# Laying the weights' word operations one a step in a fused attention, gate and mixing kernel

## Chip, cores and metric

The kernel runs on one core of a Trainium2 chip. The metric is the device time of one execution in microseconds, as the median of several runs. One profiled execution stands beside them, and every row below is from it.

## What is computed

Three blocks, one behind the other, on a batch of 2 with 768 positions. The change lies in the first, whose work includes preparing weights for the second.

```python
# attention, 8 heads of 64: rows see only keys of their own hash bucket
mask = q_bucket[:, :, :, None] == k_bucket[:, :, None, :]
scores = np.where(mask, scale * q @ k.T, -1e9)
attn = softmax(scores) @ v
# gate: 5 taps along the sequence, conv_w of 5 x 512; w_val, w_out 512 x 512
gate = sigmoid(sum(conv_w[k] * xp[:, k:k + S, :] for k in range(5)))
x = gate * (x @ w_val) @ w_out
# mixing: the real part of a 2-D DFT, a layer norm, an MLP of 512 x 2048 x 512
u = x + real(fft(fft(x, axis=1), axis=2))
out = u + relu(norm(u) @ w_ch1) @ w_ch2
```

The weights arrive as 64-bit floats. The kernel makes of each a high part of fewer bits and a low part, both 32-bit, with integer operations on the two 32-bit words of each number; these are called word operations here.

## The kernel before, in words

**Pairs and steps.** The attention walks over 8 pairs (batch, two heads). A pair has 12 steps, one for each tile of 128 query rows of its two heads, so the loop at L811 has `NT` = 96 steps `n` and two more, with `p, i = divmod(n, 12)`. A step issues, in this order: six transposes of the softmax tile `n` (`p_transpose`, L593), on some steps with two q/k transposes of a later pair beside them (`beside`, L701); the four matmuls of the scores of tile `n + 3` (L557); their clamp with the row minimum on VectorE (L568); the tile's high part on ScalarE (L601) and its low part on VectorE (L605), and the q/k low part (L709) if q/k stood beside; the products with the values (`pv`, L616); the exponential of tile `n + 2` on ScalarE (L575); and then small work: bits of the hash buckets in steps 4 and 5 (L443, L453, L454), copies of outputs on odd steps (L631), values and the convolution on GpSimd.

**What sets the order.** Nothing is rescheduled: each engine takes its instructions in the order in which this loop writes them, so a piece of small work stands where the loop calls it, and everything behind it on its engine waits. The scores have one PSUM tile (`pss`, L310), so the scores of one step can be written only when the clamp of the step before has read them.

**The word operations.** `words_split` (L262) prepares a half of a 128-row chunk of `w_val` (`val_weights`, L785) or of `w_out`'s first chunk (`out_half`, L797), 128 x 256 numbers. It makes five calls, `step0` to `step4`: two operations on VectorE (L271, L272); one (L275); one on ScalarE (L278) and two on VectorE (L279, L280); one on VectorE (L283); one on ScalarE (L286). Their PSUM tile comes from `psm`, which has one buffer and also serves the bits and the conv weights' transpose. The loop (L884 to L890) lays one call a step on steps 6 to 10 of a pair; on steps 7 to 11 in pair 0, and on 0 to 4 in the last. The halves of `w_out` follow in the last pair, steps 5 to 10 (L897 to L908). Each also starts the load of the next `w_val` half (`val_load`).

**The conv weights.** `conv_weights` (L759) converts the 20 x 128 numbers of `conv_w` in the first steps and adds the two parts on VectorE (`whole`, L769); `turn` transposes them on TensorE (L773) and copies them out on VectorE (L774). `CW` (L33) says the step of each of its eight calls.

Of the kernel before, what the change touches and what calls it, by code (L numbers as in the profile page):

```python
# [13 lines left out]
ALU = mybir.AluOpType  # L14
# [15 lines left out]
KSCALE = -0.125  # L30
BIG = 2.0 ** 33

CW = (2, 3, 4, 4, 5, 6, 7, 12)  # L33

WARM = (18, 3, 4)
CLAMP = BIG / 4
# [68 lines left out]
def block_kernel(  # L105
# [4 lines left out]
    nc = tc.nc  # L110
# [65 lines left out]
    def run(steps):  # L176
        for x in steps:
            x()
# [38 lines left out]
    def val_matmul(b, a, c, pv_):  # L217
        xh, xl = xsplit[b, a]
        n = 0
        for w, x in ((wvh, xh), (wvl, xh), (wvh, xl)):  # L220
            for ic in range(NC):
                nc.tensor.matmul(  # L222
                    pv_, w[:, ic, c * P : (c + 1) * P], x[:, ic, :],
                    start=n == 0, stop=n == 3 * NC - 1,
                )
                n += 1
# [33 lines left out]
    wo_raw, wo_h, wo_l = {}, [None] * NC, [None] * NC  # L260

    def words_split(raw, dst_h, dst_l, b, a, g):  # L262

        n = raw.shape[1]
        words = raw.bitcast(I32).rearrange("p (n two) -> p n two", two=2)
        lo, hi = words[:, :, 0], words[:, :, 1]
        a, g = a.bitcast(I32), g.bitcast(I32)
        e = ap4.tile([P, DM], I32, tag="cve", name="cv")[:, :n]

        def step0():  # L270
            nc.vector.tensor_scalar(a, hi, 0x7FFFFE00, None, op0=ALU.bitwise_and)  # L271
            nc.vector.tensor_scalar(g, hi, 0x1FF, 15, op0=ALU.bitwise_and, op1=ALU.logical_shift_left)  # L272

        def step1():
            nc.vector.scalar_tensor_tensor(g, lo, 17, g, op0=ALU.logical_shift_right, op1=ALU.bitwise_or)  # L275

        def step2():
            nc.scalar.activation(a, a, AF.Relu, scale=8.0, bias=col[:, b : b + 1])  # L278
            nc.vector.scalar_tensor_tensor(a, hi, -(2 ** 31), a, op0=ALU.bitwise_and, op1=ALU.bitwise_or)  # L279
            nc.vector.tensor_scalar(e, a, -(2 ** 23), None, op0=ALU.bitwise_and)  # L280

        def step3():
            nc.vector.scalar_tensor_tensor(dst_l, g, 2.0 ** -35, e.bitcast(F32), op0=ALU.mult, op1=ALU.mult)  # L283

        def step4():
            nc.scalar.copy(dst_h, a.bitcast(F32))  # L286

        return [step0, step1, step2, step3, step4]

    def half_weights(raw, dst_h, dst_l, b):  # L290
        t = psm.tile([P, DM], F32, tag="m", name="cvp")
        n = DM // 2
        return words_split(raw, dst_h, dst_l, b, t[:, :n], t[:, n:])
# [8 lines left out]
    def attention(es):  # L302
# [10 lines left out]
        NPR = len(pairs)  # L313
# [47 lines left out]
        def qk_tile(i, pl=ap3):  # L361
            return pl.tile([P, 2, S], F32R, tag=f"qk{i}", name="qk")
# [396 lines left out]
        def conv_weights():  # L759
            cwr, cwh, cwl, cw = cws  # L760
            
            def words_of(n, x):
                c0 = (2 + "aeg".index(x)) * P
                return conv_tmp[:, c0 : c0 + n].bitcast(I32)

            steps = from64(words_of, cwr, lambda: (cwh, cwl), parts=20)

            def whole():
                nc.vector.tensor_tensor(cw, cwh, cwl, op=ALU.add)  # L769

            def turn():
                cwp = psm.tile([P, HS], F32, tag="m", name="cwp")
                nc.tensor.transpose(cwp[:, :20], cw, ident[:20, :20])  # L773
                nc.vector.tensor_copy(cwt, cwp[:, :20].rearrange("p (k c) -> p k c", k=5))  # L774

            return steps + [whole, turn]
# [3 lines left out]
        def val_load(i):  # L780
            c, h = divmod(i, 2)
            wv_raw[i] = ap4.tile([P, DM // 2], I64, tag="wvr", name="wvr", bufs=2)
            nc.sync.dma_start(wv_raw[i], w_val[c * P : (c + 1) * P, h * DM // 2 : (h + 1) * DM // 2])

        def val_weights(i):  # L785
            c, h = divmod(i, 2)
            cs = slice(h * DM // 2, (h + 1) * DM // 2)
            return half_weights(wv_raw[i], wvh[:, c, cs], wvl[:, c, cs], 3)

        def out_tile(i):  # L790
            t = qk_tile((0, 2, 1)[i]).rearrange("p a s -> p (a s)")
            for x in range(3):
                c, part = divmod(3 * i + x, 2)
                if c < NC:
                    (wo_h, wo_l)[part][c] = t[:, x * DM : (x + 1) * DM]

        def out_half(i):  # L797
            cs = slice(i * DM // 2, (i + 1) * DM // 2)
            return half_weights(wo_raw[0][:, cs], wo_h[0][:, cs], wo_l[0][:, cs], 4)
# [3 lines left out]
        def val_early(n, early):  # L803
            c = n - NT + 3
            tail.append(early[:, c % 2, :HS])
            val_matmul(0, 0, c, tail[c])

        convs = [(b, c, i) for b, c in pairs[: NPR - 1] for i in range(9)]
        start()
        NT = 12 * NPR  # L810
        for n in range(NT + 2):  # L811
            p, i = divmod(n, 12)
# [32 lines left out]
            if p + 1 < NPR:  # L845
                prep_step(p + 1, i)
            if n == CW[0]:
                conv = conv_weights()
            run(conv.pop(0) for x in CW if x == n)
            if i == 2 and p + 2 < NPR:  # L850
# [4 lines left out]
            last = p == NPR - 1  # L855
# [25 lines left out]
            elif n == NT - 2:  # L881
                norm_spread(p)

            at = 0 if last else 7 if p == 0 else 6  # L884
            if p < NPR and at <= i < at + 5:
                if i == at:
                    wsteps = val_weights(p)
                    if p + 1 < NPR:
                        val_load(p + 1)
                wsteps[i - at]()  # L890
            for _ in range(1 if n >= NT - 16 else 5 * n // 6 - 5 * (n - 1) // 6):
                if convs and n < NT and n >= min(12 * (4 * convs[0][0] + convs[0][1]) + 22, NT - 6):
                    conv_pool(*convs.pop(0), conv_tmp)
            if p == 6 and i in (2, 6):
                out_load(i // 6)

            if last and i == 5:  # L897
                for x in range(2):
                    out_tile(x)
                osteps = out_half(0)  # L900
            elif last and i == 9:
                osteps = out_half(1)
                osteps.pop(0)()
            if last and 5 <= i < 11:
                osteps.pop(0)()
                if i in (8, 10):
                    run(osteps)
                    osteps = []  # L908
            if p == 5 and i == 9:
                again(pool_copy, 0, slice(0, NC))  # L910
            elif last and i == 6:
# [8 lines left out]
            if NT - 3 <= n < NT + 1 and n != NT - 1:  # L920
                val_early(n, early)
# [20 lines left out]
    with ExitStack() as es:  # L942
        ps, late, convs = attention(es)
# [70 lines left out]
    def mixing(es):  # L1014
# [53 lines left out]

        def chunk(c):
            a, g_ = (x.tile([P, DM], F32, tag=y, name="cvp") for x, y in ((psm, "m"), (pso, "o")))  # L1070
            return words_split(wo_raw[c], wo_h[c], wo_l[c], 4, a, g_)

        def gated(c):
            gate(0, 1, c, late[c], stay=True)
# [5 lines left out]
        for c in range(3):  # L1080
            x_low(1, 0, c)
        w = chunk(1)
        w[0]()
        w[1]()
# [19 lines left out]
        for x in convs:  # L1104
            conv_pool(*x, xT[0][:, 3, :S])
        w = chunk(2)
        w[0]()
        w[1]()
# [325 lines left out]
```

## Time and profile before

| what | us |
|---|---|
| median of 3 runs | 617.57 |
| lowest and highest | 617.46, 617.91 |
| the profiled execution | 617.87 |
| its span | 616.1 |
| TensorE busy in the span | 604.9 |
| VectorE busy | 444.3 |
| ScalarE busy | 358.7 |
| GpSimd busy | 264.8 |

The span is the time between the first and the last instruction; what lies around it is 1.8 us here. A busy TensorE is not TensorE at its peak, since matmuls overlap and their ends are modelled: in the rows a group of transposes or scores lasts into the next group, so the spacing of starts is what to read. Idle time of an engine counts only where another waits for it.

### The profile page before, as it was taken

To read this page: it belongs to the slowest core of one execution; us is meant where nothing else is said; L and a number is where in the kernel's file an instruction comes from. 1 tells how busy PE (TensorE), PEld (TensorE's weight loads), DVE (VectorE), ACT (ScalarE), POOL (GpSimd) and SP (SyncE) were. 2 spreads that over 40 slices of the span, in tenths; PEclk is the share of its full clock that TensorE was granted. 3 is DMA by queue.
4 is the path that set the end of the run, shared out by engine and by line. 5 is a ranking of instruction groups with operands and counts; after the bars stand their busy time and mean duration, and the time that the engine had idled before them with its cause. 6 is when DMAs were issued, how large, how long until landed. Compare 5 with 4: busy or idle time off the path is not lost.

```text
span 616.1 us, 10295 instructions
## 1 busy us (share of the span) xinstructions
PE 604.9 (98%) x3711; PEld 538.6 (87%) x3711; DVE 444.3 (72%) x850; ACT 358.7 (58%) x712; POOL 264.8 (43%) x273
## 2 busy tenths in 40 slices
PE   8999999999999999999999999999999999999997
PEld 7889999999999899998899888888888888888885
DVE  4999999999999997998669787888885411111113
ACT  5988899998999887844624355555665111111121
POOL 7241669687888798792350633233321000000000
PEclk9999999999999999999999999999999999999999
DMA  6966676768686720261100244343440200000002
GB/s 133 215 151 155 162 155 163 164 155 184 153 190 167 174 70 19 73 231 69 41 29 2 68 138 132 108 136 118 126 133 1 103 0 1 1 0 1 1 1 103
DMA packets 52557, 62.01 MB, mean 101 GB/s; under 512 B 28704, under 2 KB 39304, under 8 KB 52250
## 3 DMA queue, kind: packets, MB, share of 16 engines
q1 hardware_dynamic: 51770, 57.81, 36.9%
q0 software_dynamic: 432, 3.55, 1.5%
q8 instruction: 29, 0.48, 0.4%
q14 instruction: 22, 0.18, 0.1%
q10 hardware_dynamic: 304, 0.01, 0.0%
HBM read 36.73 MB, written 3.19 MB: 65 GB/s over the span
## 4 chain that ended last, share of the span: by engine, by line
PE 81%; DVE 14%; issue 2%; ACT 2%; DMA 1%; POOL 0%; SPq 0%; DVEq 0%; ACTq 0%; POOLq 0%
PE pf L1341 20%; PE acc L1351 20%; PE sp L557 9%; PE op L616 8%; PE ptp L593 7%; PE ps L1158 4%; DVE ptl L605 3%; DVE sd L568 3%; PE ps L222 3%; PE ps L1222 3%; PE bp L443 1%; PE late L222 1%; PE ptp L701 1%; PE ps L1193 1%; PE early L222 1%
## 5 line engine op out<-in xcount | busy, mean ns | idle before, releaser
L1351 PE MATMUL acc<-w,hid 128*128 128x512 f32 x576 | 137.4, 391 | 0.0
L1351 PEld LDWEIGHTS acc<-w,hid 128*128 128x128 f32 x576 | 105.5, 188 | 20.1
L1344 DVE SCALAR_TENSOR_TENSOR hid<-pf,hid 128x512 fp32r<-128x512 f32 (+1 forms) x62 | 33.4, 556 | 120.6 <-ACT hid L1343 120.6
L1341 PE MATMUL pf<-uth,w 128*128 128x512 f32 (+1 forms) x496 | 97.2, 337 | 0.1
L568 DVE TENSOR_SCALAR_CACHE_REDUCE sd<-sp 128x768 f32<-128x768 f32 x96 | 91.3, 952 | 7.4 <-PE sp L557 6.9
L1343 ACT ACTIVATE hid<-pf 128x512 fp32r<-128x512 f32 (+1 forms) x62 | 28.9, 488 | 115.2 <-PE pf L1341 115.2
L557 PE MATMUL sp<-qk 128*128 128x512 f32 (+1 forms) x384 | 91.4, 360 | 4.5 <-DVE sd L568 3.7
L605 DVE TENSOR_TENSOR ptl<-ptp,pth 128x768 fp32r<-128x768 f32 x96 | 91.5, 953 | 4.2 <-ACT pth L601 3.8
L1341 PEld LDWEIGHTS pf<-uth,w 128*128 128x128 f32 x496 | 78.9, 188 | 15.6 <-DVE hid L1344 1.9
L575 ACT ACTIVATE sd<-sd,nm 128x768 f32<-128x768 f32 x96 | 90.2, 940 | 1.5 <-DVE sd L568 1.5
L601 ACT CAST pth<-ptp 128x768 fp32r<-128x768 f32 x96 | 77.1, 803 | 17.7 <-PE ptp L701 8.7
L593 PE MATMUL ptp<-ident,sd 128*128 128x128 f32 x576 | 78.5, 272 | 0.2 <-ACT sd L575 0.2
L162 POOL TENSOR_TENSOR w<-cv 128x512 fp32r<-128x512 f32 x31 | 40.4, 1302 | 88.7 <-DVE cv L157 74.4
L616 PE MATMUL op<-pth,v 128*128 128x256 f32 x288 | 73.7, 282 | 0.2 <-ACT xc L631 0.2
L616 PE MATMUL op<-ptl,v 128*128 128x256 f32 x288 | 73.7, 286 | 0.0
L557 PEld LDWEIGHTS sp<-qk 128*128 128x128 f32 x384 | 58.2, 189 | 14.2 <-DVE sd L568 7.9
L593 PEld LDWEIGHTS ptp<-ident,sd 128*128 128x128 f32 x576 | 65.8, 140 | 1.1 <-ACT sd L575 0.5
L616 PEld LDWEIGHTS op<-pth,v 128*128 128x128 f32 x288 | 54.2, 188 | 4.5 <-ACT xc L631 0.4
L616 PEld LDWEIGHTS op<-ptl,v 128*128 128x128 f32 x288 | 54.2, 188 | 0.3
L1341 PE MATMUL pf<-utl,w 128*128 128x512 f32 (+1 forms) x248 | 53.1, 335 | 0.0
L241 POOL TENSOR_TENSOR g<-g,conv_tmp 128x768 f32<-128x768 f32 x27 | 46.7, 1728 | 1.6
L149 ACT ACTIVATE cv<-cv,col 128x512 int32<-128x512 int32 x32 | 23.2, 725 | 40.3 <-DVE cv L146 40.3
(214 smaller groups left out, 984.9 us busy)
## 6 DMA issues: line engine op xcount, KB each, us to landing
raw<-in_moe_w_ch_dram SPq DMA_DIRECT2D x32, 512.0 KB
qk<-ht SPq DMA_DIRECT2D x60, 192.0 KB
qk<-lt SPq DMA_DIRECT2D x30, 192.0 KB
rqk<-in_q_dram SPq DMA_DIRECT2D x16, 192.0 KB
rqk<-in_k_dram SPq DMA_DIRECT2D x16, 192.0 KB
rv<-in_v_dram SPq DMA_DIRECT2D x8, 384.0 KB
out_dram<-o SPq DMA_DIRECT2D x12, 256.0 KB
xm<-xc SPq DMA_DIRECT2D x15, 192.0 KB
```

The costliest lines, as they stand in the source:

```text
L162: nc.gpsimd.tensor_tensor(dst()[1], fold(g.bitcast(F32)), fold(e.bitcast(F32)), op=ALU.mult)
L241: nc.gpsimd.tensor_tensor(dst, dst, tmp, op=ALU.add)
L557: nc.tensor.matmul(sp[:, cs], q2[i][:, m, qi * P : (qi + 1) * P], k2[i][:, m, cs], start=m == order[0], stop=m == order[1])
L568: nc.vector.tensor_scalar(sd[n], sp, CLAMP, None, op0=ALU.min, op1=ALU.min, accum_out=st[p]["nm"][:, n % 12 : n % 12 + 1],)
L575: nc.scalar.activation(sd[n], sd[n], AF.Exp, bias=st[p]["nm"][:, i : i + 1], scale=-1.0, accum_out=st[p]["sums"][:, i : i + 1],)
L593: nc.tensor.transpose(tp[:, r // 3, c0 : c0 + P], sd[n][:, r * P : (r + 1) * P], ident)
L601: nc.scalar.copy(p_parts(n)[0], tp)
L605: nc.vector.tensor_tensor(lo, tp, f32(ho), op=ALU.subtract)
L616: nc.tensor.matmul(po[kb], v3[:, r, c0 : c0 + P], pt[kb][x][:, r, :], start=r == 0 and x == 0, stop=r == R - 1 and x == 1,)
L1341: nc.tensor.matmul(pf, w[:, c, :], x[:, c, cs], start=n == 0, stop=n == 3 * NC - 1)
L1344: nc.vector.scalar_tensor_tensor(hl[:, cs], pf, 0.0, f32(hh)[:, cs], op0=ALU.max, op1=ALU.subtract)
L1351: nc.tensor.matmul(acc, x[:, ts_], w, start=f == 0 and n == 0, stop=f == NF - 1 and n == 2)
```

## The change

`words_split` returns its eight operations by name in place of five calls. In the attention they are laid by a table: for each half a list of steps and names. Halves 1 to 5 begin in step 5 of their pair and end in step 13, which is step 1 of the next pair: `magnitude` 5, `rebias` and `rest` 6, `rest_low` 7, `sign` 8, `high` 10, `exponent` 12, `low` 13. Half 0 goes from step 7 to step 14. Halves 6 and 7 and the two of `w_out` follow each other from step 77 to step 94, one operation of VectorE a step, with the last `w_out` half pressed into two steps. `rebias` (ScalarE) now stands ahead of `rest`, and `high` (ScalarE) ahead of `exponent` or `low` where both are in one step. The later chunks of `w_out`, behind the attention, keep the five calls (`in_five`).

The addition of the conv weights moves from VectorE to GpSimd, and their transpose from step 12 to step 15.

```diff
-CW = (2, 3, 4, 4, 5, 6, 7, 12)
+CW = (2, 3, 4, 4, 5, 6, 7, 15)
...
-        def step2():
+        def rebias():
             nc.scalar.activation(a, a, AF.Relu, scale=8.0, bias=col[:, b : b + 1])
+
+        def sign():
             nc.vector.scalar_tensor_tensor(a, hi, -(2 ** 31), a, op0=ALU.bitwise_and, op1=ALU.bitwise_or)
...
+    def in_five(steps):
+        groups = ("magnitude", "rest"), ("rest_low",), ("rebias", "sign", "exponent"), ("low",), ("high",)
+        return [lambda x=x: run(steps[k] for k in x) for x in groups]
...
             def whole():
-                nc.vector.tensor_tensor(cw, cwh, cwl, op=ALU.add)
+                nc.gpsimd.tensor_tensor(cw, cwh, cwl, op=ALU.add)
...
+        words = [
+            [(7, "magnitude"), (8, "rebias rest"), (9, "rest_low"), (11, "sign"), (12, "exponent"), (13, "low"), (14, "high")]
+        ]
+        for p in range(1, NPR - 2):
+            words.append(
+                [(12 * p + i, x) for i, x in (
+                    (5, "magnitude"), (6, "rebias rest"), (7, "rest_low"), (8, "sign"), (10, "high"), (12, "exponent"), (13, "low"),
+                )]
+            )
+        for n in (12 * NPR - 19, 12 * NPR - 13):
+            words.append(
+                [(n + i, x) for i, x in enumerate(
+                    ("magnitude", "rebias rest", "rest_low", "sign", "high exponent", "low")
+                )]
+            )
+        n = 12 * NPR - 7
+        words.append(
+            [(n + i, x) for i, x in enumerate(("magnitude", "rebias rest", "rest_low", "sign", "high exponent low"))]
+        )
+        words.append([(n + 4, "magnitude rest"), (n + 5, "rebias rest_low sign exponent high low")])
...
-            at = 0 if last else 7 if p == 0 else 6
-            if p < NPR and at <= i < at + 5:
-                if i == at:
-                    wsteps = val_weights(p)
-                    if p + 1 < NPR:
-                        val_load(p + 1)
-                wsteps[i - at]()
+            words_step(n)
...
-            if last and i == 5:
-                for x in range(2):
-                    out_tile(x)
-                osteps = out_half(0)
-            elif last and i == 9:
-                osteps = out_half(1)
-                osteps.pop(0)()
-            if last and 5 <= i < 11:
-                osteps.pop(0)()
-                if i in (8, 10):
-                    run(osteps)
-                    osteps = []
```

**VectorE, pair 1, before.** The words start behind step 6's low part (`ptl`) and go to step 9; `sd` is a clamp, `lt` a q/k low part, `cvp`, `cv` and `wvl` are word operations. Names in brackets are what a row waits for.

```order
L271 TENSOR_SCALAR cvp<-wvr 128x256 [waits DVE_49]
L272 TENSOR_SCALAR cvp<-wvr 128x256 [waits DVE_49]
L568 TENSOR_SCALAR sd,nm<-sp 128x768 [waits PE_49]
L605 TENSOR_TENSOR ptl<-ptp,pth 128x6x128 [waits Activation_49]
L275 SCALAR_TENSOR_TENSOR cvp<-wvr,cvp 128x256 [waits DVE_49]
L568 TENSOR_SCALAR sd,nm<-sp 128x768 [waits PE_49]
L605 TENSOR_TENSOR ptl<-ptp,pth 128x6x128 [waits Activation_49]
L279 SCALAR_TENSOR_TENSOR cvp<-wvr,cvp 128x256 [waits Activation_49]
L280 TENSOR_SCALAR cv<-cvp 128x256 [waits DVE_49]
L568 TENSOR_SCALAR sd,nm<-sp 128x768 [waits PE_49]
L605 TENSOR_TENSOR ptl<-ptp,pth 128x6x128 [waits Activation_49]
L709 SCALAR_TENSOR_TENSOR lt<-ptp,col,ht 128x256 [waits DMAHW7_49,DMAHW0_49]
```

The same place of the change, from step 5's comparison of bits (L467) to step 8's `sign` (L283):

```order
L467 TENSOR_TENSOR bits<-bp,bits 64x384 [waits Activation_49]
L271 TENSOR_SCALAR cvp<-wvr 128x256 [waits DVE_49]
L581 TENSOR_SCALAR sd,nm<-sp 128x768 [waits PE_49]
L618 TENSOR_TENSOR ptl<-ptp,pth 128x6x128 [waits Activation_49]
L274 TENSOR_SCALAR cvp<-wvr 128x256 [waits Activation_49]
L581 TENSOR_SCALAR sd,nm<-sp 128x768 [waits PE_49]
L618 TENSOR_TENSOR ptl<-ptp,pth 128x6x128 [waits Activation_49]
L277 SCALAR_TENSOR_TENSOR cvp<-wvr,cvp 128x256 [waits DVE_49]
L581 TENSOR_SCALAR sd,nm<-sp 128x768 [waits PE_49]
L618 TENSOR_TENSOR ptl<-ptp,pth 128x6x128 [waits Activation_49]
L283 SCALAR_TENSOR_TENSOR cvp<-wvr,cvp 128x256 [waits DVE_49]
```

No two word operations stand between two clamps any more; the second, `rest` (L274), waits for ScalarE, where its forerunner L272 waited for VectorE.

**ScalarE, steps 92 to 94, before.** `pth` is a high part of a softmax tile, `sd` an exponential, `xc` an output copy; the two L286 are the high parts of the `w_out` halves.

```order
L601 CAST pth<-ptp 128x6x128 [waits PE_49,Activation_49]
L575 ACTIVATE sd,sums<-sd,nm 128x768 [waits DVE_49]
L286 CAST qk<-cvp 128x256 [waits DMAHW6_49,DMAHW7_49,DMAHW3_49,DVE_49]
L601 CAST pth<-ptp 128x6x128 [waits PE_49]
L575 ACTIVATE sd,sums<-sd,nm 128x768 [waits Activation_49]
L631 COPY xc<-op 128x256 [waits DMAHW5_49,PE_49,Pool_49]
L601 CAST pth<-ptp 128x6x128 [waits PE_49,Activation_49]
```

The same place of the change:

```order
L614 CAST pth<-ptp 128x6x128 [waits PE_49,Activation_49]
L588 ACTIVATE sd,sums<-sd,nm 128x768 [waits DVE_49]
L614 CAST pth<-ptp 128x6x128 [waits PE_49]
L588 ACTIVATE sd,sums<-sd,nm 128x768 [waits DVE_49,Activation_49]
L644 COPY xc<-op 128x256 [waits DMAHW5_49,PE_49,Pool_49]
L292 CAST qk<-cvp 128x256 [waits DMAHW6_49,DMAHW7_49,DMAHW3_49,DVE_49]
L614 CAST pth<-ptp 128x6x128 [waits PE_49,Activation_49]
```

The `w_out` high part (now L292) went behind the next softmax tile, its exponential and the output copy.

## Rows read from the trace of the kernel before

**Rows 1.** Busy us by engine in two stretches; then TensorE's clock, DMA share, GB/s.

```profile
core 0: us, PE busy (x) PEld busy (x) DVE busy (x) ACT busy (x) POOL busy (x), PEclk, DMA share, GB/s
90.00:120.00 30.00, 29.71 (x228) 28.14 (x227) 28.69 (x54) 27.05 (x57) 24.21 (x24) 1.00 0.72 161
...
203.00:238.00 35.00, 34.14 (x253) 31.58 (x252) 33.81 (x66) 29.66 (x59) 31.01 (x28) 1.00 0.41 100
```

**Rows 2.** The chain of waits, one pair: start us, us on the chain, what.

```profile
91.06 0.96 DVE ptl L605
92.02 0.35 DVE cvp L271
...
92.39 0.43 DVE cvp L272
...
93.73 0.97 PE sp L557 x4
...
120.52 0.35 DVE cvp L271
```

**Rows 3.** Timeline of TensorE, transposes of steps: start us, us, engine, line, operation.

```profile
90.57 0.82 PE L593 MATMUL ptp<-ident,sd 128*128 128x128 f32 x6
...
92.63 0.82 PE L593 MATMUL ptp<-ident,sd 128*128 128x128 f32 x6
...
95.30 0.82 PE L593 MATMUL ptp<-ident,sd 128*128 128x128 f32 x6
...
97.58 0.82 PE L593 MATMUL ptp<-ident,sd 128*128 128x128 f32 x6
...
104.51 0.82 PE L593 MATMUL ptp<-ident,sd 128*128 128x128 f32 x6
```

**Rows 4.** Timeline of VectorE in the same pair.

```profile
92.72 0.95 DVE L568 TENSOR_SCALAR_CACHE_REDUCE sd<-sp 128x768 f32<-128x768 f32 x1
...
93.59 0.95 DVE L605 TENSOR_TENSOR ptl<-ptp,pth 128x768 fp32r<-128x768 f32 x1
94.46 0.42 DVE L275 SCALAR_TENSOR_TENSOR cvp<-wvr,cvp 128x256 int32<-128x256 int32 x1
94.79 0.95 DVE L568 TENSOR_SCALAR_CACHE_REDUCE sd<-sp 128x768 f32<-128x768 f32 x1
...
96.54 0.42 DVE L279 SCALAR_TENSOR_TENSOR cvp<-wvr,cvp 128x256 int32<-128x256 int32 x1
96.99 0.42 DVE L280 TENSOR_SCALAR cv<-cvp 128x256 int32<-128x256 int32 x1
...
99.08 0.47 DVE L709 SCALAR_TENSOR_TENSOR lt<-ptp,col,ht 128x256 fp32r<-128x256 f32 x1
99.47 0.41 DVE L283 SCALAR_TENSOR_TENSOR wvl<-cvp,cv 128x256 fp32r<-128x256 int32 x1
```

**Rows 5.** Timelines of TensorE and VectorE in pair 0, steps 8 to 14.

```profile
34.27 0.82 PE L593 MATMUL ptp<-ident,sd 128*128 128x128 f32 x6
...
47.29 0.23 PE L773 MATMUL cwp<-ident,cwr 20*128 20x20 f32 x1
...
49.80 0.82 PE L593 MATMUL ptp<-ident,sd 128*128 128x128 f32 x6
...
35.74 0.71 DVE L769 TENSOR_TENSOR cwr<-cwr 20x128 f32<-20x128 f32 x1
```

**Rows 6.** Timeline of VectorE, first and last of fifteen clamps, steps 78 to 92.

```profile
204.06 0.96 DVE L568 TENSOR_SCALAR_CACHE_REDUCE sd<-sp 128x768 f32<-128x768 f32 x1 [0.22 <-PE sp L557]
...
236.09 0.95 DVE L568 TENSOR_SCALAR_CACHE_REDUCE sd<-sp 128x768 f32<-128x768 f32 x1
```

**Rows 7.** Timelines of ScalarE and TensorE, steps 92 to 94; idle before in brackets.

```profile
238.28 0.37 ACT L286 CAST qk<-cvp 128x256 fp32r<-128x256 f32 x1 [1.63 <-DVE qk L283]
...
240.59 0.38 PE L616 MATMUL op<-pth,v 128*128 128x256 f32 x1 [0.19 <-ACT xc L631]
```

**Rows 8.** Timeline of ScalarE: an exponential in step 6 of a pair, a `rebias`.

```profile
90.11 0.94 ACT L575 ACTIVATE sd<-sd,nm 128x768 f32<-128x768 f32 x1
...
222.66 0.43 ACT L278 ACTIVATE cvp<-cvp,col 128x256 int32<-128x256 int32 x1
```

More of the change, by code (lines that the diff above doesn't have):

```diff
@@ L268, in words_split, with magnitude, rest, rest_low @@
         e = ap4.tile([P, DM], I32, tag="cve", name="cv")[:, :n]
-        def step0():
+        def magnitude():
             nc.vector.tensor_scalar(a, hi, 0x7FFFFE00, None, op0=ALU.bitwise_and)
+        def rest():
             nc.vector.tensor_scalar(g, hi, 0x1FF, 15, op0=ALU.bitwise_and, op1=ALU.logical_shift_left)
-        def step1():
+        def rest_low():
             nc.vector.scalar_tensor_tensor(g, lo, 17, g, op0=ALU.logical_shift_right, op1=ALU.bitwise_or)
-        def step2():
+        def rebias():
             nc.scalar.activation(a, a, AF.Relu, scale=8.0, bias=col[:, b : b + 1])
+        def sign():
             nc.vector.scalar_tensor_tensor(a, hi, -(2 ** 31), a, op0=ALU.bitwise_and, op1=ALU.bitwise_or)
+        def exponent():
             nc.vector.tensor_scalar(e, a, -(2 ** 23), None, op0=ALU.bitwise_and)
-        def step3():
+        def low():
             nc.vector.scalar_tensor_tensor(dst_l, g, 2.0 ** -35, e.bitcast(F32), op0=ALU.mult, op1=ALU.mult)
-        def step4():
+        def high():
             nc.scalar.copy(dst_h, a.bitcast(F32))
-        return [step0, step1, step2, step3, step4]
+        return dict(
+            magnitude=magnitude, rest=rest, rest_low=rest_low, rebias=rebias, sign=sign, exponent=exponent,
+            low=low, high=high,
+        )
+    def in_five(steps):
+        groups = ("magnitude", "rest"), ("rest_low",), ("rebias", "sign", "exponent"), ("low",), ("high",)
+        return [lambda x=x: run(steps[k] for k in x) for x in groups]
     def half_weights(raw, dst_h, dst_l, b):
@@ L806, in val_early, with words_step @@
             val_matmul(0, 0, c, tail[c])
+        words = [
[16 more added lines that the diff above has]
+            [(n + i, x) for i, x in enumerate(("magnitude", "rebias rest", "rest_low", "sign", "high exponent low"))]
+        )
+        words.append([(n + 4, "magnitude rest"), (n + 5, "rebias rest_low sign exponent high low")])
+        parts = {}
+        def words_step(n):
+            for i, plan in enumerate(words):
+                for at, names in plan:
+                    if at != n:
+                        continue
+                    if at == plan[0][0]:
+                        if i == NPR:
+                            for x in range(2):
+                                out_tile(x)
+                        parts[i] = val_weights(i) if i < NPR else out_half(i - NPR)
+                        if i + 1 < NPR:
+                            val_load(i + 1)
+                    run(parts[i][x] for x in names.split())
         convs = [(b, c, i) for b, c in pairs[: NPR - 1] for i in range(9)]
@@ L1070, in chunk @@
             a, g_ = (x.tile([P, DM], F32, tag=y, name="cvp") for x, y in ((psm, "m"), (pso, "o")))
-            return words_split(wo_raw[c], wo_h[c], wo_l[c], 4, a, g_)
+            return in_five(words_split(wo_raw[c], wo_h[c], wo_l[c], 4, a, g_))
         def gated(c):
```

## The prediction

> **What bounds the kernel now.** I read the busy times by stretch first. In the attention's steady stretch TensorE is busy 29.71 of 30 us and VectorE 28.69; from 203 to 238 us it is 34.14 and 33.81 of 35, with GpSimd at 31.01 [rows 1]. Two engines are full, so a mean cannot say which ends a step. The chain of waits can: at 91 us it leaves TensorE for VectorE, goes through the low part of a softmax tile, through two word operations (0.35 and 0.43) and the clamp behind them, and returns with the scores at 93.73 [rows 2]. The scores have one PSUM tile, so TensorE cannot compute the next ones before the clamp has read the last ones. The reader should see this: the word operations are on the path only because several stand in one step, ahead of a clamp.
>
> How much that costs is the spacing of TensorE's transposes, one group a step. A plain step takes 2.06 us (90.57 to 92.63), one with q/k transposes beside 2.28 (95.30 to 97.58). From 92.63 to 104.51 stand two plain steps and three of the others, which would be 2 x 2.06 + 3 x 2.28 = 10.96; they take 11.88 [rows 3]. So about 0.9 us of each pair is TensorE waiting for VectorE, and a pair takes 28.5 (the same word operation on the chain at 92.02 and 120.52 [rows 2]).
>
> VectorE's own step, back to back: clamp to low part 0.87 (92.72 to 93.59), low part to the next operation 0.87 (to 94.46), and one word operation 0.33 (94.46 to 94.79). That is 2.07, with one word operation, against TensorE's 2.06: balanced. Two in a step cost about 0.8, since the second waits for the first to end (96.54 to 96.99; 0.35, 0.02 and 0.43 on the chain); a q/k low part ahead adds 0.39 (99.08 to 99.47) [rows 4]. Now the steps of pairs 1 to 5 with words have two, one, two and one of them, the last beside a q/k low part, and then none for eight steps.
>
> **The change, part by part.**
> Pairs 1 to 5. No word operation is removed; the same six on VectorE and two on ScalarE are laid over steps 5 to 13. Steps 6, 7 and 8 get one each: 0.87 + 0.87 + 0.33 = 2.07, which TensorE's 2.06 to 2.28 nearly covers. Step 5 and step 12 get one; step 5 is a bits step, in which TensorE has four more matmuls and VectorE is early, and step 12 has 2.07 against 2.06. Step 13 has one beside a q/k low part: 2.07 + 0.39 = 2.46 against 2.28, 0.18 late. That lateness is paid out of slack: the scores wait for a clamp that starts 1.01 us before them (92.72 to 93.73 [rows 2, 4]), and scores take 0.97 before their clamp, so a step of 2.28 can take a clamp 0.3 late. I leave 0.1 of the 0.9. Gain 5 x 0.8 = 4.0; ends 5 x 0.35 (a lone operation costs 0.45) and 5 x 0.9.
>
> Pair 0. From 34.27 to 49.80 stand one plain step, three with q/k transposes, one plain with the conv weights' transpose (0.23 in its row, 0.2 of TensorE's time), and one more with q/k: 2.06 + 3 x 2.28 + 2.26 + 2.28 = 13.44, against 15.53, so 2.1 is lost. The addition of the conv weights (0.71 on VectorE) stood in front of two word operations in one step [rows 5]; it leaves VectorE. Now each step has at most one word operation, but steps 9, 11 and 13 have it beside a q/k low part (2.46), and step 11 precedes a plain step. I leave 0.3. The transpose costs TensorE its 0.2 either way, three steps later. Gain 1.8; ends 1.0 and 2.1. On GpSimd the addition is bounded by nothing and by about the 0.71 that it took on VectorE; GpSimd is free there, as it was waiting for transfers, and nobody but the later transpose reads it.
>
> The last two pairs. From step 78 to step 92 the clamps go from 204.06 to 236.09: 14 steps in 32.03 [rows 6]. No q/k work stands here, so TensorE needs 2.06 a step and VectorE now 2.07 or 2.08 in each: 14 x 2.08 = 29.1. That is 2.9 less; I take 2.7, as a reciprocal and one more lone operation stand in this stretch too. Ends 1.0 (0.45 each, giving 14 x 2.19 = 30.7, and a little lost) and 3.2 (TensorE alone).
>
> The last three steps. ScalarE's high part of the first w_out half now stands ahead of the low part. Before, ScalarE sat 1.63 us idle until VectorE's low part was out, with a softmax tile queued behind, and TensorE's next products then waited for ScalarE, by 0.19 in the row [rows 7]. Now VectorE waits for ScalarE instead, at a place where it has nothing urgent. The second half's six operations in step 94 hold the last softmax tile as they did. Ends 0 and 1.6; I take 0.4, nearer to TensorE's own idle.
>
> New waits. The order of the built program shows two: the second word operation, `rest`, now waits for ScalarE's `rebias`, and `exponent` for ScalarE's `high` where both stand in one step. Behind them queue the next clamp and TensorE's scores. ScalarE starts its exponential at 90.11, for 0.94, and a `rebias` takes 0.43 [rows 8]: done by 91.5, while VectorE comes to `rest` after its low part at 92.02 [rows 2]. 0.5 to spare; cost nothing, at worst the 0.43 each. The load of the next w_val half goes out one step earlier on SP, still behind the bits; it has twelve steps to land. The PSUM tile of the words is held into step 13; the bits that need it come in step 16, three steps (over 6 us) later.
>
> Sum: 4.0 + 1.8 + 2.7 + 0.4 = 8.9. The profiled execution took 617.87 (span 616.1), so 609.0; the median of the runs shown, 617.57, lies 0.3 lower, so **608.7**. Everything behind the attention is taken to move up whole, since its loads are started by its own steps.
>
> **The rivals.**
> A lone operation costs its full duration. The row shows 0.42 of duration but 0.33 to the next start [rows 4], so here the next one begins before the last has ended. If alone it held VectorE for all 0.42, each step that VectorE ends would be 0.09 longer: 14 x 0.09 = 1.3 in the last pairs, 3 x 0.09 x 5 = 1.35 in pairs 1 to 5, 0.3 in pair 0. Time 608.7 + 3.0 = 611.7. The trace speaks against it wherever no wait stands between. The Trainium skill, "VectorE: DVE Perf Modes", section "The DRAIN you can't avoid", says that the next operation does not start until the pipe is empty, and that only the number of operations counts; by that rule the time would be this rival's, and laying the same operations out would gain less.
>
> GpSimd becomes the bound at the end. It has 3.99 us idle in 35 [rows 1] and the stretch is to shrink by 2.7, so it fits, but barely: its additions wait for transfers, and the reciprocal of the last sums waits for it with the last tiles behind. If it holds, the 2.7 and the 0.4 are lost: 611.8.
>
> ScalarE is late. Spare is 0.5 where it is on time. If its queue runs later, each of ten `rest` operations stops VectorE for up to 0.43: 4.3 lost, 613.0.
>
> Slower. One word operation a step is worse than several in a few steps if a lone one keeps the clamp away for long, since nearly every step then pays. The addition of the conv weights, small and alone, held it 0.71 [rows 5]. At 0.6 a word operation, the last 14 steps take 14 x 2.34 = 32.8, over today's 32.03, and in a pair steps 6 to 8 lose 0.28 each and step 13 (2.73 for 2.28) some 0.3 beyond its slack, 1.15 where 0.9 is lost now: 0.8 + 5 x 0.25 = 2.1 slower, 619.7. It decides where 14 x (1.74 + x) passes 32.03, at x = 0.55, and a little below it in the pairs. Against it: 0.33 in the row of one that stands alone before a clamp [rows 4].
>
> Nothing gained. If something with a pace of its own, the q/k transfers or GpSimd, sets a pair's 28.5, TensorE finds a new wait: 617.2. The chain through a pair names neither [rows 2].
>
> **How the numbers follow.** Forecast 0.66 (own range 607.6 to 610.2); full duration 0.12; GpSimd 0.08; ScalarE 0.05; nothing gained 0.04; slower 0.05. 0.2% is 1.2 us, about what a measurement can tell from no change. Faster: 0.66 + 0.12 + 0.08 + 0.05 = 0.91; within 0.04; slower 0.05. The range goes from 607.4 (all of TensorE's waits gone) to 612.2, over the first two rivals.
>
> **What would show it.** In the profile after, a step of the last pairs should be 2.07 to 2.10 by the clamps, a pair near 27.7; TensorE's waits for the clamp in a pair should nearly vanish; the chain should have no word operation in pairs 1 to 5; VectorE's wait for ScalarE in `rest` and `exponent` should be zero. A step of 2.2 or more with one word operation, or a VectorE wait on ScalarE's `rebias`, makes the forecast wrong; a step of 2.3 makes it slower.

## The result, and the profile after

The changed kernel took **610.99 us** (median of 4 runs, 610.8 to 612.43) against 617.74 for the kernel before in the same session: a ratio of 0.9891, 95% interval 0.9875 to 0.9908. The forecast was 608.7, with a range of 607.4 to 612.2. The profiled execution took 610.95 (span 609.1, before 616.1), so the gain to compare with the forecast's 8.9 is 6.9. The time alone does not speak for the forecast's own mechanism: it lies outside the 607.6 to 610.2 given for that, and nearer to the rivals at 611.7 and 611.8. The traces have to decide.

Line numbers of the attention are 13 higher than before: the clamp is L581, the low part L618, the scores L570. Busy time by engine in the two stretches of [rows 1]:

```profile
90.00:120.00 30.00, 30.00 (x232) 28.70 (x231) 29.29 (x56) 27.80 (x58) 25.01 (x24) 1.00 0.73 164
203.00:238.00 35.00, 35.00 (x265) 33.69 (x265) 33.39 (x66) 29.47 (x59) 32.03 (x28) 1.00 0.40 99
```

TensorE is now busy through both. The chain of waits says the same. Where [rows 2] left TensorE for two word operations, it now stays on TensorE (three pieces of a step, in a stretch in which all are TensorE's):

```profile
91.17 0.66 PE ptp L606 x6
91.83 0.71 PE sp L570 x4
92.54 0.77 PE op L629 x6
```

VectorE's step in the last pairs, by start, duration and operation, answers [rows 4] and [rows 6]:

```profile
199.31 0.43 DVE L271 TENSOR_SCALAR cvp<-wvr 128x256 int32<-128x256 int32 x1
199.64 0.95 DVE L581 TENSOR_SCALAR_CACHE_REDUCE sd<-sp 128x768 f32<-128x768 f32 x1
...
200.51 0.95 DVE L618 TENSOR_TENSOR ptl<-ptp,pth 128x768 fp32r<-128x768 f32 x1
201.38 0.42 DVE L274 TENSOR_SCALAR cvp<-wvr 128x256 int32<-128x256 int32 x1
201.71 0.95 DVE L581 TENSOR_SCALAR_CACHE_REDUCE sd<-sp 128x768 f32<-128x768 f32 x1
...
228.60 0.42 DVE L277 SCALAR_TENSOR_TENSOR cvp<-wor,cvp 128x256 int32<-128x256 int32 x1
228.93 0.95 DVE L581 TENSOR_SCALAR_CACHE_REDUCE sd<-sp 128x768 f32<-128x768 f32 x1
```

0.87 + 0.87 + 0.33 = 2.07, clamp to clamp, as forecast; a word operation of 0.42 lets the clamp start after 0.33. By the clamps, term by term:

| stretch | before | after | gain | forecast |
|---|---|---|---|---|
| clamp of step 7 to that of 18 (pair 0) | 27.67 | 26.88 | 0.79 | 1.8 |
| 18 to 78 (pairs 1 to 5) | 142.50 | 138.94 | 3.56 | 4.0 |
| 78 to 92 (last pairs) | 32.03 | 29.29 | 2.74 | 2.7 |
| 92 to the first product of w_val's second part | 15.25 | 15.54 | -0.29 | 0.4 |

With 0.07 ahead of step 7 that is 6.87, which is how much earlier that product starts (251.34 and 244.47). Behind the attention nothing is lost. The last pairs are as forecast and pairs 1 to 5 are 0.4 short; pair 0 is 1.0 short and the end 0.7, and both show a wait that the profile of before did not. In pair 0 it is in step 9 (VectorE, TensorE, SyncE and GpSimd, idle time before an operation in brackets):

```profile
36.00 0.95 DVE L581 TENSOR_SCALAR_CACHE_REDUCE sd<-sp 128x768 f32<-128x768 f32 x1
...
38.89 0.96 DVE L581 TENSOR_SCALAR_CACHE_REDUCE sd<-sp 128x768 f32<-128x768 f32 x1 [0.73 <-PE sp L570]
...
37.91 0.94 PE L570 MATMUL sp<-qk 128*128 128x512 f32 x4 [0.38 <-DVE ptl L618]
...
34.68 1.55 SPq L448 DMA_DIRECT2D qk<-bits  x2
...
34.62 0.45 POOL L782 TENSOR_TENSOR cwr<-cwr 20x128 f32<-20x128 f32 x1
```

The clamp of step 8 comes at 36.00 where it came at 37.16, and the next one is 2.89 behind it, for want of scores. The profile says that the scores waited for VectorE's low part. These are the first scores of pair 1, though, and need its sign bits, which SyncE sends off at 34.68. At the end, ScalarE and TensorE ([rows 7]):

```profile
237.01 0.37 ACT L292 CAST qk<-cvp 128x256 fp32r<-128x256 f32 x1 [2.05 <-DVE cv L286]
237.40 1.28 ACT L954 ACT_TABLE_LOAD   x1
...
238.81 0.78 ACT L614 CAST pth<-ptp 128x768 fp32r<-128x768 f32 x1
...
227.93 0.94 PE L570 MATMUL sp<-qk 128*128 128x512 f32 x4
...
240.06 0.36 PE L629 MATMUL op<-pth,v 128*128 128x256 f32 x1
240.63 0.39 PE L629 MATMUL op<-ptl,v 128*128 128x256 f32 x1 [0.21 <-DVE ptl L618]
```

The last high part of the softmax (238.81) stands behind the table load, its low part behind that, and TensorE waits at 240.06: 0.57 to the next product, where the kernel before takes 0.29 (247.21 to 247.50). The row at 227.93 is the last scores; in the kernel before they are these:

```profile
234.59 0.94 PE L557 MATMUL sp<-qk 128*128 128x512 f32 x4
```

### The profile page after: what moved, and what is told of

Same layout as the page of the kernel before. It is cut to its first block, busy times and chain, and to the rows that moved or that the text cites. A ratio compares the mean times of both kernels' runs of the same rounds, so it can differ in the third digit from the quotient of the medians.

```text
span 609.1 us, 10268 instructions
## 1 busy us (share of the span) xinstructions
PE 600.7 (99%) x3711; PEld 537.5 (88%) x3711; DVE 441.4 (72%) x849; ACT 357.7 (59%) x712; POOL 265.3 (44%) x274
## 4 chain that ended last, share of the span: by engine, by line
PE 90%; DVE 6%; ACT 2%; issue 1%; DMA 1%; POOL 0%; SPq 0%; ACTq 0%; POOLq 0%
PE pf L1372 21%; PE acc L1382 20%; PE op L629 10%; PE sp L570 10%; PE ptp L606 9%; PE ps L1189 5%; PE ps L222 3%; PE ps L1253 3%; PE ps L1224 1%; PE bp L456 1%; PE late L222 1%; PE ptp L714 1%; PE early L222 1%; DVE ptl L618 1%; PE idle L369 1%
## 5 line engine op out<-in xcount | busy, mean ns | idle before, releaser
L581 DVE TENSOR_SCALAR_CACHE_REDUCE sd<-sp 128x768 f32<-128x768 f32 x96 | 91.0, 948 | 4.8 <-PE sp L570 3.1
L618 DVE TENSOR_TENSOR ptl<-ptp,pth 128x768 fp32r<-128x768 f32 x96 | 91.5, 953 | 2.3 <-ACT pth L614 2.0
L570 PE MATMUL sp<-qk 128*128 128x512 f32 (+1 forms) x384 | 91.1, 359 | 1.7 <-DVE sd L581 0.8
L570 PEld LDWEIGHTS sp<-qk 128*128 128x128 f32 x384 | 58.2, 189 | 8.3 <-DVE sd L581 1.6
```

The costliest lines, as they stand in the source:

```text
L570: nc.tensor.matmul(sp[:, cs], q2[i][:, m, qi * P : (qi + 1) * P], k2[i][:, m, cs], start=m == order[0], stop=m == order[1])
L581: nc.vector.tensor_scalar(sd[n], sp, CLAMP, None, op0=ALU.min, op1=ALU.min, accum_out=st[p]["nm"][:, n % 12 : n % 12 + 1],)
L618: nc.vector.tensor_tensor(lo, tp, f32(ho), op=ALU.subtract)
```

## The experiments

Each was run beside the kernel before on the same chip; times are medians of 4 to 12 runs. Where a difference is a few tenths, it is read from the trace, counted from a common clamp, since medians of this kernel do not resolve it.

### The wait in step 9: conv_alone, add_vector, bits_early, bits_two_queues

conv_alone is the kernel before with one line of the change:

```diff
-                nc.vector.tensor_tensor(cw, cwh, cwl, op=ALU.add)
+                nc.gpsimd.tensor_tensor(cw, cwh, cwl, op=ALU.add)
```

> The kernel before, with only the conv weights' addition on GpSimd (its transpose stays in step 12). Theory (in step 9 of pair 0 TensorE's scores wait for the transfers of pair 1's sign bits, which land near 37.8 us, so what VectorE gains in step 8 is cut there): the clamp of step 8, at 37.16 in the kernel before, comes near 36.5, but the scores of step 9, at 38.17 before, come no earlier than 37.9; time 0.2 to 0.3 below the kernel before. Rival (VectorE alone set that step, the addition's whole 0.64 comes back): scores of step 9 near 37.5, time 0.6 to 0.7 below. Second rival (the addition costs GpSimd, which scales the sign bits and copies the values there): the time is that of the kernel before or above it.

617.26 against 617.61, ratio 0.9997 (0.9987 to 1.0006). From the clamp of step 7 to that of step 9 it takes 5.08 (33.29 to 38.37) where the kernel before takes 5.34 and the change 5.07. VectorE came 0.63 earlier, and 0.26 of it was used. Here the profile names the transfer:

```profile
34.15 1.56 SPq L435 DMA_DIRECT2D qk<-bits  x2
...
37.39 0.94 PE L557 MATMUL sp<-qk 128*128 128x512 f32 x4 [0.38 <-DMA qk<-bits]
```

add_vector is the change with that line undone (`nc.vector` again), all else as it is.

> The change with the conv weights' addition back on VectorE, all else as in the change. Theory of the transfers: the addition delays the clamp of step 8 from 36.00 to about 36.65 us, which still ends before the transfers land near 37.8; scores of step 9 stay within 0.1 of 37.91 and the time within 0.2 of the change's. Rival (VectorE sets that step): scores of step 9 near 38.5, time 0.6 above the change's.

Clamp 7 to clamp 9: 5.07 again (33.51 to 38.58), although the addition took VectorE 0.70 and the clamp of step 8 came 2.81 after that of 7 in place of 2.18.

```profile
34.37 1.55 SPq L448 DMA_DIRECT2D qk<-bits  x2
...
37.61 0.93 PE L570 MATMUL sp<-qk 128*128 128x512 f32 x4 [0.38 <-DMA qk<-bits]
...
35.36 0.70 DVE L782 TENSOR_TENSOR cwr<-cwr 20x128 f32<-20x128 f32 x1
...
37.20 0.94 DVE L618 TENSOR_TENSOR ptl<-ptp,pth 128x768 fp32r<-128x768 f32 x1
```

The scores start at 37.61 while the low part runs until 38.14, so they do not wait for it. They start 3.24 after SyncE's first issue here and in conv_alone, 3.23 in the change. **The bound is the transfers of the sign bits**. The profile of the change names the low part, which there ended 0.09 before the scores start (36.87 + 0.95 = 37.82); add_vector shows that they do not need it. To the clamp of step 92 add_vector takes what the change takes (195.13 and 195.11 from the clamp of step 7). Its time, 611.75 (610.75 to 612.47; ratio 0.9902, 0.9887 to 0.9916), misses the expectation by 0.6, with two of its five runs as fast as the change's. The profiled execution lost 0.9 at the end, on GpSimd (VectorE's reciprocal of the last sums, and the GpSimd rows ahead of it):

```profile
202.59 0.54 SPq L655 DMA_DIRECT2D xm<-xc  x1
...
209.61 1.84 POOL L657 TENSOR_TENSOR xm<-xc,xm 64x768 f32<-64x768 f32 x1 [3.02 <-DMA xm<-xc]
...
235.88 0.20 POOL L661 TENSOR_SCALAR sums<-sums 128x12 f32<-128x12 f32 x1
...
236.12 0.23 DVE L665 RECIPROCAL rinv<-sums 128x12 f32<-128x12 f32 x1 [0.81 <-POOL sums L661]
```

One transfer, issued at 202.59, let GpSimd sit 3.02 idle (1.46 in the change); it then worked through to the sums without a pause, and VectorE waited for it. In the change the sums are out at 234.74 and the reciprocal starts at 235.51, so GpSimd had about 0.8 to spare. Why that transfer took longer in this execution was not settled.

bits_early moves pair 1's sign bits a step forward:

```diff
-            at = 5 if first else 4
+            at = 4
```

> The change with pair 1's sign bits a step earlier (steps 4 and 5 in place of 5 and 6), so that their two transfers are issued some 2.5 us earlier. Theory of the transfers: the 2.89 us from the clamp of step 8 to that of step 9 falls to 2.3 to 2.5, the scores of step 9 no longer wait; time 0.4 to 0.6 below the change's, near 610.4. Rival (those scores wait for VectorE's low part, which the trace names): the 2.89 stay, time as the change's. Second rival (the bits' PSUM tile, shared with the q/k transposes of step 4, makes TensorE wait in step 4 instead): the 2.89 falls, a step before grows by as much, time as the change's.

Slower than the change, which no expectation had: 612.58, ratio 0.9918 (0.9905 to 0.9930). The step in question fell to 2.28, so the transfers' bound is gone, but the clamp of step 5 comes 5.82 after that of step 4 in place of 3.18. That is the second rival's place, at 2.64 and not the 0.6 that it priced: TensorE's projection (`bp`) sits behind step 4's q/k parts.

```profile
27.92 0.44 PE L456 MATMUL bp<-ht,ph 128*128 128x384 f32 x1 [1.42 <-DVE lt L418]
```

bits_two_queues sends one of the two transfers from GpSimd:

```diff
-                nc.sync.dma_start(f32(x)[0:NR, 1, :], bits[r : r + NR, :])
+                e = nc.gpsimd if p == 1 and j == 0 and r else nc.sync
+                e.dma_start(f32(x)[0:NR, 1, :], bits[r : r + NR, :])
```

> The change with one of the two transfers of pair 1's sign bits (steps 0 to 6 of pair 0, second image of k) issued by GpSimd, right behind its scaling of the bits, in place of SyncE, so that the two go at once. Theory of the transfers: both land 0.5 to 0.8 earlier than 37.8 us, scores of step 9 follow at 37.2 to 37.4, and the step from the clamp of 8 to that of 9 falls from 2.89 to 2.3 to 2.4; time 0.5 below the change's. Rival (GpSimd's own issue takes as long as SyncE's two, about 1.5): the 2.89 stay and the time is the change's; GpSimd's values run later and no one waits for them. Rival (the wait is for VectorE's low part): the 2.89 stay although the transfers land earlier.

610.73 (610.59 to 610.95), ratio 0.9887 (0.9873 to 0.9900). The step is 2.80 for 2.89: 0.09 won, so the first rival has the outcome nearly right, but not the reason. GpSimd's issue takes 0.72, not 1.5; it starts at 34.64, 0.3 behind SyncE's, and the scores start 2.85 after it, at 37.49.

### Pairs 1 to 5: magnitude_late, pairs_old

```diff
-                    (5, "magnitude"), (6, "rebias rest"), (7, "rest_low"), (8, "sign"), (10, "high"), (12, "exponent"), (13, "low"),
+                    (6, "magnitude"), (7, "rebias rest"), (8, "rest_low"), (9, "sign"), (10, "high"), (12, "exponent"), (13, "low"),
```

> The change with the first word operations of pairs 1 to 5 one step later: magnitude in step 6, rebias and rest in 7, rest_low in 8, sign in 9; the other three where they are. Theory (what the change leaves of a pair's loss, 27.78 against 27.57 summed from TensorE's steps, comes from magnitude standing behind the comparison of the bits in step 5, which makes the next clamp 0.14 late): steps 5 to 6 fall from 2.90 to 2.76, step 9 takes 2.46 on VectorE for 2.28 on TensorE out of slack; pairs of 27.6, time 0.7 below the change's (0.4 to 1.0). Rival (the lateness moves to step 9, which has its word operation beside a q/k low part): pairs stay at 27.8, time within 0.2 of the change's. Second rival: step 9 and step 13 together use up the slack, pairs of 27.95, time 0.8 above.

The first rival's number for a pair is right, but not its place, step 9. Step 5 to 6 falls from 2.91 to 2.76 as meant, but 6 to 7 grows from 2.06 to 2.20, and a pair takes 27.80 (88.50 to 116.30) where the change takes 27.78. VectorE had sat idle for scores just before the clamp at 116.30. The low part behind that starts 1.00 after the clamp, where it otherwise starts 0.87 after, and the word operation comes on top: 1.00 + 0.87 + 0.33 = 2.20. The high part that the low part needs was out at 116.45, in ScalarE's row, so this is no wait for ScalarE; what the 0.13 is, the trace does not say.

```profile
116.30 0.96 DVE L581 TENSOR_SCALAR_CACHE_REDUCE sd<-sp 128x768 f32<-128x768 f32 x1 [0.23 <-PE sp L570]
...
117.30 0.96 DVE L618 TENSOR_TENSOR ptl<-ptp,pth 128x768 fp32r<-128x768 f32 x1
118.17 0.42 DVE L271 TENSOR_SCALAR cvp<-wvr 128x256 int32<-128x256 int32 x1
118.50 0.95 DVE L581 TENSOR_SCALAR_CACHE_REDUCE sd<-sp 128x768 f32<-128x768 f32 x1
...
115.65 0.80 ACT L614 CAST pth<-ptp 128x768 fp32r<-128x768 f32 x1 [0.24 <-PE ptp L606]
```

So the first word operation behind the bits costs about 0.15 a pair in either of the two steps; other places were not run. The time was 611.91 (ratio 0.9906, 0.9893 to 0.9919), 0.9 above the change's. In the trace the first output leaves only 0.2 later than in the change (602.69 and 602.47); the rest lies in what follows, since from that issue to the end of the span it takes 7.6 here and 6.6 in the change. This 1.0 of the profiled execution is not explained.

pairs_old puts the five old steps back in pairs 1 to 5:

```diff
-                    (5, "magnitude"), (6, "rebias rest"), (7, "rest_low"), (8, "sign"), (10, "high"), (12, "exponent"), (13, "low"),
+                [(12 * p + 6 + i, x) for i, x in enumerate(("magnitude rest", "rest_low", "rebias sign exponent", "low", "high"))]
```

> The change with the word operations of pairs 1 to 5 in the old five steps (6 to 10, two, one, two, one and none on VectorE), pair 0 and the last pairs as in the change. Theory (the losses of the stages add): pairs of 28.50, 3.6 above the change's time, 614.5. Rival (what one stage gains is partly given back where the next begins, or later): 2.5 or less above.

615.19, ratio 0.9957 (0.9945 to 0.9970), 4.2 above the change's median. In the trace 18 to 78 takes 142.64 for 138.94, and the first output leaves 3.63 later (606.10 and 602.47): the expected 3.6. The outputs' end takes 7.6 from there again, so the median's 4.2 is more than the stage gives. The chain of waits has the two word operations again:

```profile
90.17 0.96 DVE ptl L618
91.13 0.35 DVE cvp L271
91.48 0.02 issue
91.50 0.43 DVE cvp L274
91.93 0.88 DVE sd L581 x2
```

### The last pairs and the end: last_old, table_early, both_mended

last_old has the old places from step 77 on (val halves in steps 78 to 82 and 84 to 88, w_out's in 89 to 92 and 93 to 94):

```diff
-        for n in (12 * NPR - 19, 12 * NPR - 13):
...
+        for n in (12 * NPR - 18, 12 * NPR - 12):
+            words.append([(n + i, x) for i, x in enumerate(("magnitude rest", "rest_low", "rebias sign exponent", "low", "high"))])
...
+        words.append([(n + i, x) for i, x in enumerate(("magnitude rest", "rest_low", "rebias sign exponent", "low high"))])
+        words.append([(n + 4, "magnitude rest rest_low"), (n + 5, "rebias sign exponent low high")])
```

> The change with the word operations from step 77 on in the old places (two, one, two, one and none in steps 78 to 82 and 84 to 88, and so on), pairs 0 to 5 as in the change. Theory (stages add): from the clamp of 78 to that of 92 32.0 in place of 29.29, and the end after it 15.25 in place of 15.54; time 2.4 to 2.5 above the change's, 613.4. Rival (the end keeps its 15.54 whatever stands before it): 2.7 to 2.8 above. Rival (part of the 2.7 was lost again behind the attention): under 2.

613.21, ratio 0.9931 (0.9917 to 0.9944), 2.2 above the change's. 78 to 92 takes 32.02, the end 15.23 (231.54 to 246.77); together, and counted from the clamp of step 0, that is 2.45 more than in the change, as the theory said. So the end depends on what stands before it: a last clamp that is late by VectorE's account is late against a TensorE that has already gone on.

table_early moves one line:

```diff
-            if n == NT - 2:
+            if n == NT - 3:
                 nc.scalar.activation(warm, warm, AF.Sigmoid)
```

> The change with the load of ScalarE's sigmoid table one step earlier (end of step 93 in place of 94), where ScalarE sits 1.24 us idle. Theory (the end of the attention lost what the softmax step gained because the last high part, 238.81 us, stands behind the second half's high part and this load, so that TensorE waits for the last low part at 240.06 to 240.63): high part near 237.4, low part near 238.2, no wait there; from the last clamp to the first product of the second w_val part 15.54 falls to 15.1 to 15.2; time 0.4 below the change's. Rival (the products after it wait for something else, ScalarE's sums or the conv's additions): TensorE's wait moves on to the sums' transposes or the next products, time within 0.1 of the change's.

In the trace as expected, 15.18 for 15.54 (228.96 to 244.14), with TensorE's products back to back; the high part started at 238.09, not 237.4, since the second half's high part was later in this execution, in which VectorE's reciprocal of the last sums waited 0.52 for GpSimd:

```profile
232.61 1.28 ACT L954 ACT_TABLE_LOAD   x1
...
238.09 0.81 ACT L614 CAST pth<-ptp 128x768 fp32r<-128x768 f32 x1
...
240.09 0.36 PE L629 MATMUL op<-pth,v 128*128 128x256 f32 x1
240.29 0.28 PE L629 MATMUL op<-ptl,v 128*128 128x256 f32 x1
```

The median, 610.92 (610.69 to 611.56; ratio 0.9891, 0.9878 to 0.9905), does not show the 0.36.

both_mended is table_early and bits_two_queues together.

> The change with table_early and bits_two_queues together. Theory (their gains in the trace, 0.36 at the end of the attention and 0.09 in step 9, add): the first product of the second w_val part 0.45 earlier than the change's, counted from the clamp of step 0; time 610.4 to 610.6. Rival (one hides the other): as the better of the two alone, 610.7 to 610.9.

610.71 (610.6 to 610.87), ratio 0.9888 (0.9874 to 0.9901). In the trace the end takes 15.17 and the step in pair 0 2.73; counted from the clamp of step 0, the first product of w_val's second part comes 0.33 earlier than in the change (227.50 and 227.83), under the 0.45. Counted the same way, table_early alone wins 0.23 (227.60) and bits_two_queues alone 0.05 (227.78), so the two add, within 0.05. It is the best in the trace, by an amount that the medians (0.3) cannot settle.

### What an operation costs: extra_word, extra_psum

Both add one word operation a step, which nobody reads, in steps 78 to 91. extra_word reads and writes SBUF; extra_psum reads a PSUM tile:

```diff
+            nc.vector.tensor_scalar(e2, hi, 0x7FFFFE00, None, op0=ALU.bitwise_and)
...
+                    if 12 * NPR - 18 <= n <= 12 * NPR - 5:
+                        parts[i]["extra"]()
```

```diff
+            nc.vector.tensor_scalar(e2, tp[:, 0, :n].bitcast(I32), 0x7FFFFE00, None, op0=ALU.bitwise_and)
```

> The change with one more word operation on VectorE in each of steps 78 to 91 (the form of magnitude, into the unused half of the exponents' tile), which nothing reads and which waits for nothing recent. Theory (an operation costs VectorE the 0.33 to the next start where it waits for no result of the one before): 14 steps of 2.40 from the clamp of 78 to that of 92, 33.6 where the change takes 29.29; time 4.3 above the change's, 615.2. Rival (each operation holds VectorE for its whole 0.42 to 0.46): steps of 2.49 to 2.53, 34.9 to 35.4, time 5.6 to 6.1 above. Rival of the kernel before (two in a step cost 0.8 because they are two, not because the second waits): 2.07 + 0.47 = 2.54 a step.

All three expectations missed: 619.37, ratio 1.0034 (1.0020 to 1.0048), slower than the kernel before. 78 to 92 took 37.53, 8.24 more than in the change or 0.59 an operation, and one lasts from 0.28 to 1.22. VectorE and GpSimd:

```profile
207.16 0.28 DVE L272 TENSOR_SCALAR cv<-wvr 128x256 int32<-128x256 int32 x1
...
216.62 0.40 DVE L278 TENSOR_SCALAR cvp<-wvr 128x256 int32<-128x256 int32 x1
216.93 1.22 DVE L272 TENSOR_SCALAR cv<-wvr 128x256 int32<-128x256 int32 x1
218.08 0.94 DVE L585 TENSOR_SCALAR_CACHE_REDUCE sd<-sp 128x768 f32<-128x768 f32 x1
...
205.11 1.83 POOL L241 TENSOR_TENSOR g<-g,conv_tmp 128x768 f32<-128x768 f32 x1
208.01 1.84 POOL L661 TENSOR_TENSOR xm<-xc,xm 64x768 f32<-64x768 f32 x1 [1.06 <-DMA xm<-xc]
...
216.16 1.85 POOL L241 TENSOR_TENSOR g<-g,conv_tmp 128x768 f32<-128x768 f32 x1
```

The one at 207.16, while GpSimd is idle (206.94 to 208.01), takes 0.28. The one at 216.93 meets a GpSimd operation that runs until 218.01, and ends 0.14 after it; ten of the fourteen end 0.14 or 0.15 after a GpSimd operation that was running when they started. The word operation ahead of that one, whose output lies in PSUM, takes 0.40 beside the same GpSimd operation. That led to the second kernel:

> The change with one more word operation on VectorE in each of steps 78 to 91, as in extra_word, but reading a PSUM tile (the step's transposed softmax tile, whose numbers nobody uses there) in place of the weights in SBUF. Theory (an operation with an operand in PSUM costs VectorE the 0.33 to the next start, whatever GpSimd does; extra_word's 0.28 to 1.22 were waits for GpSimd's running operation, because both of its operands lie in SBUF): steps of 2.40, 33.6 to 33.9 from the clamp of 78 to that of 92 where the change takes 29.29 and extra_word 37.53; time 4.3 to 4.6 above the change's, 615.4. Rival (full duration, 0.42 to 0.46 each): 34.9 to 35.5, time 5.6 to 6.2 above. Rival (any second operation in a step is held by GpSimd): 37.5, time 619.4.

615.27, ratio 0.9959 (0.9946 to 0.9973), and 33.76 from 78 to 92: 2.41 a step. Fourteen extra operations cost 4.47, 0.32 each. The theory is right in both parts:

```profile
217.88 0.42 DVE L281 SCALAR_TENSOR_TENSOR cvp<-wvr,cvp 128x256 int32<-128x256 int32 x1
218.21 0.41 DVE L272 TENSOR_SCALAR cv<-ptp 128x256 int32<-128x256 int32 x1
218.54 0.94 DVE L585 TENSOR_SCALAR_CACHE_REDUCE sd<-sp 128x768 f32<-128x768 f32 x1
```

## Why the prediction was right, and where its terms were off

The mechanism was right. That the time lies in the range is owed in part to its width: it was drawn over two rivals, and the forecast's own mechanism was short by 2 of 8.9. Word operations were on the path because two stood ahead of one clamp; laid one a step they leave it, and the chain of pairs 1 to 5 has none. pairs_old and last_old give their stages' time back, 3.7 and 2.7 in the trace.

- **The price of a lone operation**, 0.33 to the next start [rows 4]: right, by the clamps of the last pairs and by extra_psum's 0.32. The rival of the full duration is refuted; at their full duration these fourteen would have cost 0.41 each. That is the rule that the prediction cites from the Trainium skill, "VectorE: DVE Perf Modes", "The DRAIN you can't avoid". The same section adds that a next operation that is not held starts earlier, which the prediction left out, and with that the traces agree. The prediction's reason for the 0.8 of two in a step, that the second waits for the first to end, is the smaller part: two cost 0.46 + 0.33 = 0.79 with that wait and 0.66 without it (217.88 to 218.54), so 0.13 is the wait and the rest is that they are two. `rest` uses nothing that `magnitude` computes; the wait is for its end. Even without it two are too many for a step, by extra_psum's 2.41 against TensorE's 2.06.
- **Last pairs**, 2.7: measured 2.74.
- **Pairs 1 to 5**, 4.0: measured 3.56. "I leave 0.1 of the 0.9" was mis-sized: about 0.2 stays, most of it because `magnitude` in step 5 stands behind the comparison of the bits, where the prediction called VectorE early (step 5 to 6 is 2.91 for 2.76). magnitude_late shows that one step later does not recover it. Step 13's lateness was paid out of slack, as the prediction said: step 13 to 14 is 2.47 for 2.29, and the steps behind it are shorter by as much.
- **Pair 0**, 1.8: measured 0.8. The step that failed is the sum that compared TensorE's and VectorE's work alone. VectorE's lateness had covered a third party, the sign bits' transfers to pair 1's first scores, and step 9 now waits 0.6 for them (2.89 for the 2.28 that bits_early takes there). conv_alone, add_vector and bits_early show it. For the remaining 0.4 the traces show two places, which no run tested apart: 0.14 is pair 1's `magnitude` in step 17 (2.90 to the next clamp, 2.76 before, 2.78 in pairs_old), and 0.25 is step 8, a plain step that takes TensorE 2.31 before and after (34.27 to 36.58, 34.19 to 36.50). The prediction had counted what that is over 2.06 into the 2.1 lost to VectorE, and the change left it as it was.
- **The end**, 0.4: measured -0.29. The wait that the prediction named was real and is gone: from the transposes to the first product TensorE takes 0.57 (232.90 to 233.47) where it took 1.00 (239.59 to 240.59). Two things ate it. The wait for the last low part grew by 0.28, since that stands behind the table load, which the prediction passed over; without the load's delay the end is 0.36 shorter (table_early). And 0.50 was counted twice: the clamp of step 92 moved by 7.16 us, its scores (234.59 before, 227.93 after) by 6.66, since the old clamp had been late for scores already there. Counted from those scores, the end gained 0.21.
- **New waits**, 0: right. VectorE did not wait for ScalarE in `rest`; in `exponent` it did once, 0.50 in step 93, when no clamp stood behind any more. The addition on GpSimd (0.45) delayed nobody.
- **GpSimd as the bound**: not in the change, but only some 0.8 off; add_vector's execution met it, and table_early's did by 0.52 without loss at the end. The rival's place was right, the reciprocal of the last sums.
- **Slower**: the price it decided on, 0.55 an operation, occurs on this chip, at 0.59 in extra_word. What excludes it here is that every word operation has an operand in PSUM. The row that it rested on, the addition's 0.71 [rows 5], is an operation with all operands in SBUF beside a working GpSimd. It ends at 36.45, 0.14 after the GpSimd operation beside it (36.31), like those of extra_word, so it looks like such a wait too; no run had the addition on VectorE without a GpSimd operation beside it:

```profile
35.29 1.02 POOL L389 TENSOR_TENSOR v<-rv,v 128x384 fp32r<-128x384 f32 x1
```

## What to carry to other kernels

When a wait for an engine is taken away, list what else must be there at that place, transfers first, and when it is there in the trace of before: here the transfers left only 0.26 us of VectorE's 0.63 to be won. Price an operation by the distance from its start to the next start, for the same placement of operands and the same neighbour, not by its duration and not by a row of another kind. Spreading small operations pays where a step has room for one; count the gain at the engine that goes on, not at the one that was late.

## What the runs showed of the hardware that was not expected

A VectorE operation of one input (128x256, 32-bit) with input and output both in SBUF takes 0.28 us with GpSimd idle and up to 1.22 us beside a GpSimd operation, until just after that one ends; the same operation with its input in PSUM takes 0.41 throughout (0.406 to 0.418 over fourteen). The Trainium skill, "SBUF — State Buffer", "Who interferes with whom", says that the two engines share a pair of SBUF ports which the first to come holds for its whole instruction. It says too that an operation with at most one SBUF input contends only in a two-port mode, and that `tensor_scalar`, the form used here, can enter one. The traces agree with the wait; that extra_word's operation ran in such a mode is inferred from the 0.28 against 0.41.

For the two transfers of the sign bits, 21 KB each, it takes 3.23 to 3.29 us in nine kernels from SyncE's first issue to the products that need both, of which the two issues take 1.55. How much of it depends on their size, no run here shows.
